# Linear attention's last stage on one core: queries against kv one head at a time, and the product with z on GpSimd

## The chip, the core and the metric

The kernel runs on one core of a Trainium2 chip. A core has TensorE (matrix products, 128 rows by 128 columns, results in PSUM), VectorE, ScalarE, GpSimd and SyncE, which here issues the DMAs. SBUF and PSUM have 128 partitions; PSUM has eight banks of 512 f32 per partition. The metric is the time of one execution on the device in microseconds, as the median over several runs. The profile comes from one execution of its own.

## The reference

One layer on x of 2048 tokens by 1024 channels: a layer norm, then a linear attention with 32 heads of 32 channels, gated by a SwiGLU block on the same normed input.

```python
q, k, v = split(xn @ wqkv)                       # 32 heads of 32
pq, pk = q @ w_phi[h], k @ w_phi[h]              # per head, 32 x 32
phi_q = concat(softmax(pq), softmax(-pq))        # 64 features a head
phi_k = concat(softmax(pk), softmax(-pk))
kv = phi_k^T v ; z = sum_s phi_k                 # per head: 64 x 32 and 64
num = phi_q @ kv ; den = phi_q . z + 1e-6
s = (num / den) heads together @ wo
g = silu((silu(xn @ w1) * (xn @ w3)) @ w2)
out = x + s * g
```

All values are f32.

## The kernel before, in words

The stages follow one another on the same engines. First x is normed, transposed and prepared, and `w_phi` is folded into the query and key weights. Then come the gate's first products (L482), the keys and values (L562), the gate's second product (L751), and last the queries with the attention and its output product. All large products are made in three passes of `float32r` (a value is split into a high part by ScalarE and a low remainder by VectorE, function `split`, L84); a few small products are in plain f32.

**Keys.** In `heads` the keys' features are made by `features` and `scaled`, and `kv` (L547) multiplies them with the values: a head takes 32 columns of the array, four heads lie side by side on the 128 rows of tokens, and the sums stand in the PSUM tile `pkv`. The values carry columns of ones, so that z comes out beside kv. `kv_out` (L594) stores both to DRAM for each half c of the heads (16 heads), in two pairs of DMAs, one for softmax(p) and one for softmax(-p).

**Turning point.** While the gate's second product ends, the kernel loads z, spread over all partitions, into `zb`, and kv into `kvs` (L821 to L831). GpSimd clears `kv_bd` and copies the 32x32 blocks onto its diagonals: four heads in a 128x128 block, for each sign s and half c. SyncE, ScalarE, VectorE and GpSimd follow the order of the program around this place (`in_order`); TensorE does not.

**Queries.** The last loop (L920) goes over 16 token tiles of 128. For tile i it projects the first half (`project_q`, 24 passes at L95), makes its features and weights (`queries`, L876), then runs `attend` (L891) for both halves of tile i-1, projects the second half of tile i, makes its `queries`, and ends tile i-1 with `finish` (L908): the product with `wo`, times the gate, plus x. The order of the instructions on each engine is not that of the text from the second tile on: `in_order()` without an argument hands it to the framework's planner, which simulates durations and places what is ready by the program's priority. Each engine runs its queue in order.

In `queries`, VectorE takes the maximum and minimum of each head (L103, L104), subtracts in both directions (L106, L107), ScalarE takes the exponent (L109), VectorE sums (L112), multiplies with z (L881, two halves s), sums again (L882), works out the reciprocals and scales e (L118). The tile e is laid out by sign s, then head.

In `attend`, four 128x128 transposes for each s put e's features on partitions (L896, into four PSUM banks with tags kv0 to kv3), ScalarE copies them to `et` (L898), and eight matmuls (L903) multiply with `kv_bd`, for each group g of four heads the two signs adding up. The result, four heads of 32 channels on the partitions for each g, stands in one bank `po`. `split` takes it to `oT`: ScalarE the high part (L86), VectorE the low part (L87). `po` has one buffer, so the second `attend` writes it when both have been taken.

Of the kernel before, what the change touches and what calls it, by code (L numbers as in the profile page):

```python
# [8 lines left out]
F = mybir.dt.float32  # L9
R = mybir.dt.float32r  # L10
AF = mybir.ActivationFunctionType
OP = mybir.AluOpType
# [5 lines left out]
P = 128  # L18
# [9 lines left out]
def tile_kernel(ctx: ExitStack, tc: tile.TileContext, x, wkT, wqT, wv, wphi, wo, w1, w3, w2, out):  # L28
# [46 lines left out]
    wk_d = [[dram.tile([P, 512], F, name=f"wk_d{c}_{k}") for k in range(ND)] for c in range(2)]  # L75
    wq_d = [[dram.tile([P, 512], F, name=f"wq_d{c}_{k}") for k in range(ND)] for c in range(2)]
    wo_d = dram.tile([D, D], F, name="wo_d")
    kv_d = dram.tile([P, 4, 4, DH], F, name="kv_d")
    z_d = dram.tile([1, 2, D], F, name="z_d")


    PASSES = ((0, 0), (0, 1), (1, 0))
# [1 line left out]
    def split(hi, lo, src, by=None):  # L84

        nc.scalar.copy(hi, src)  # L86
        (by or nc.vector).tensor_sub(lo, src, hi.bitcast(F))  # L87
# [28 lines left out]
    def scaled(e, by):  # L116
        e3 = e.rearrange("p s (h f) -> p (s h) f", f=DH)
        nc.vector.tensor_mul(e3, e3, by.unsqueeze(2).to_broadcast([P, H, DH]))  # L118
# [475 lines left out]
    def kv_out(c, pkv):  # L594
        kva = work.tile([P, 8, DH], F, name="kva", tag="w")
        zs = small.tile([P, 8], F, name="zs")
        nc.scalar.copy(kva, pkv[:, :, :DH])
        nc.vector.tensor_copy(zs, pkv[:, :, DH])
        for s in range(2):
            nc.sync.dma_start(kv_d[:, 2 * s + c], kva[:, 4 * s:4 * s + 4])  # L600
            nc.sync.dma_start(z_d[0, s, c * 512:(c + 1) * 512].rearrange("(g p) -> p g", p=P), zs[:, 4 * s:4 * s + 4])

    for d, b, t in hs:
        store_h(d, b, t)
# [36 lines left out]
    def stage(k):  # L641
        return ra.tile([P, 4, 512], F, name=f"ra{k % 2}")
# [126 lines left out]
    for r, new in enumerate(steps):  # L769
        kb, i = new or (NKB, 0)  # L770
        end = kb == NKB - 1
        if new is None:
            in_order(ENG.SP, ENG.Activation, ENG.DVE, ENG.Pool)
        if kb + 1 < NKB:
            if i == 2:
                rw = b_load(kb + 1)
            elif i == 3:
                t2 = [b_start(rw, 0)]
            elif i == 4:
                t2.append(b_start(rw, 1))  # L780
            elif i == 5:
                bos[kb + 1] = b_prep(rw, t2, BNAMES[:1], {})
            elif i == 6:
                b_prep(rw, t2, BNAMES[1:2], bos[kb + 1])
        parts = first
        if r + 1 < len(steps) - 1:
            first = a_first(*steps[r + 1])
        bank = {}
        for b, an, bn in TURN:
            if an in FIRST:  # L790
                if new:
                    product(kb, i, bank, parts[2], b, an, bn)
                    if i + 1 == len(pairs) and not end and an == "A11":
                        b_prep(rw, t2, ["T2"], bos[kb + 1])
            elif old:
                product(*old, banks, second, b, an, bn)
                if new and i == 0 and an in ("S3", "S4"):
                    b_prep(rw, t2, ["B22" if an == "S3" else "T4"], bos[kb])
                if not new:
                    k = 2 * (BNAMES.index(bn) - 2)  # L800
                    load_wo(k)
                    load_wo(k + 1)
        if new:
            second = a_second(*parts)
            if i + 1 == len(pairs):
                if end:
                    for k in range(4, 8):
                        load_r(wq, (1, k), wq_d[1][k])
                    for k in range(2):
                        load_wo(k)  # L810
                else:
                    b_prep(rw, t2, ["T1", "T3"], bos[kb + 1])


        if end:
            if i:
                gate(*pairs[i - 1])
            if 0 < i < 5:
                load_r(wq, (1, i - 1), wq_d[1][i - 1])
                split_r(wq[1, i - 1])  # L820
            if i == 2:  # L821
                zb = stage(0)
                nc.sync.dma_start(zb, z_d.rearrange("o s (c n) -> o (s c) n", c=2).to_broadcast([P, 4, 512]))
                kvs = work.tile([P, 4, 4, DH], F, name="kvs", tag="w")
                nc.sync.dma_start(kvs, kv_d)
                kv_bd = stage(1)
                nc.gpsimd.memset(kv_bd, 0.0)
            if 2 < i < 7:
                for j in range(4):
                    sl = slice(32 * j, 32 * j + 32)  # L830
                    nc.gpsimd.tensor_copy(kv_bd[sl, i - 3].rearrange("p (g d) -> p g d", d=P)[:, :, sl], kvs[sl, i - 3])  # L831
            if i == 4:
                close("acca")
                wqp = pool("wq0", 1, side="right")
                for k in range(ND):
                    load_r(wq, (0, k), wq_d[0][k], wqp.tile([P, 2, 512], R, name=f"wq0_{k}"))
            if i == 6:
                xf = load_q(0)
            if 4 < i:
                for k in range(3 * (i - 5), min(3 * (i - 4), ND)):  # L840
                    split_r(wq[0, k])
        old, banks = new, bank
# [31 lines left out]
    in_order(ENG.SP)  # L874

    def queries(p, c):  # L876
        e = acc_late.tile([P, 2, 512], F, name="e", tag="acc0", bufs=3)
        r, rf = features(e, small, p)
        ez = acc_late.tile([P, 2, 512], F, name="ez", tag="acc1", bufs=3)
        for s in range(2):  # L880
            nc.vector.tensor_mul(ez[:, s], e[:, s], zb[:, 2 * s + c])  # L881
        nc.vector.tensor_reduce(rf[:, 1, :], ez.rearrange("p s (h f) -> p (s h) f", f=DH), axis=AX.X, op=OP.add)  # L882
        nc.vector.tensor_mul(rf[:, 1, :], rf[:, 1, :], rf[:, 0, :])
        den = small.tile([P, 16], F, name="den")
        nc.vector.scalar_tensor_tensor(den, r[:, 1, 0, :], 1e-6, r[:, 1, 1, :], op0=OP.add, op1=OP.add)
        nc.vector.reciprocal(den, den)
        nc.vector.tensor_mul(r[:, 2], r[:, 0], den.unsqueeze(1).to_broadcast([P, 2, 16]))
        scaled(e, rf[:, 2, :])
        return e

    def attend(c, e):  # L891
        eT = []
        for s in range(2):
            pt = ps.tile([P, 4, P], F, name="pt2", tag=f"kv{2 * c + s}", bufs=1)
            for g in range(4):
                nc.tensor.transpose(pt[:, g, :], e[:, s, g * P:(g + 1) * P], ident)  # L896
            et = work.tile([P, 4, P], F, name="et", tag="w")
            nc.scalar.copy(et, pt)  # L898
            eT.append(et)
        po = ps.tile([P, 4, P], F, name="po", tag="tr", bufs=1)  # L900
        for g in range(4):
            for s in range(2):
                nc.tensor.matmul(po[:, g, :], kv_bd[:, 2 * s + c, g * P:(g + 1) * P], eT[s][:, g, :], start=s == 0, stop=s == 1)  # L903
        oT = wp.tile([P, 4, 2, P], R, name="oT", bufs=2)
        split(oT[:, :, 0, :], oT[:, :, 1, :], po)
        return oT

    def finish(i, oT):  # L908
# [71 lines left out]
```

## Time and profile before

| | |
|---|---|
| time, median of 3 runs | 2517.87 us (2516.3 to 2518.39) |
| the profiled execution | 2517.11 us, of which the profile's span is 2515.2 us |
| TensorE busy | 2443.6 us, 97% of the span |
| VectorE, ScalarE, GpSimd busy | 1738.6, 903.9, 596.6 us |
| TensorE's clock granted | 0.995 over the span |
| stage of queries and attention | about 2064 us to the end |

Times in the profile are microseconds from the span's start. PE is TensorE's matmul part and PEld its loading of weights, DVE is VectorE, ACT ScalarE, POOL GpSimd, SPq SyncE's queue of DMA issues. A row of the timeline has its start, its length, engine, line, operation, the tile written and those read, shapes and the number of instructions merged into it; square brackets hold idle time ahead of it and what ended that. A matmul's length holds the way through the array, so lengths of neighbouring rows overlap and starts tell more than lengths. A plain f32 matmul shows as two records. A busy TensorE need not be at its peak rate.

### The profile page before, as it was taken

Reading aid. Unit: us, or ns where it says so; the run is one execution under the profiler, and the core shown is the slowest. Engines: PE = TensorE matmul, PEld = TensorE weight load, DVE = VectorE, ACT = ScalarE, POOL = GpSimd, SP = SyncE. Lnnn points to the kernel's source line nnn. Section 1 sums busy time; section 2 is a strip of 40 time slices with the busy share of each in tenths; the row PEclk is TensorE's granted clock in tenths of the full one; section 3 lists DMA queues with packets and bytes.
Section 4 is the critical chain, followed back from the end, with each engine's and each line's share of the span. In section 5 each row is a group of like instructions: output and inputs, shape, how many; then the busy total and the mean of one; then the engine's idle time right before and its main releaser. Section 6 shows DMA issues by size and latency. Waiting matters only on the chain.

```text
span 2515.2 us, 34167 instructions
## 1 busy us (share of the span) xinstructions
PE 2443.6 (97%) x13136; PEld 2018.4 (80%) x13136; DVE 1738.6 (69%) x2635; ACT 903.9 (36%) x1593; POOL 596.6 (24%) x468
## 2 busy tenths in 40 slices
PE   6999999999999999999999989999999999999999
PEld 5888788888788888887887877888877877888887
DVE  8576766764444444443555568999999989777775
ACT  6455444433333333331111125443333453222221
POOL 1244444432222232220000002223333220100100
PEclk9999999999999999999999999999999999999999
DMA  8779887765632322338769623222122372222221
GB/s 298 235 247 296 286 249 258 249 215 173 195 105 80 101 80 72 93 138 327 268 193 328 210 86 85 92 84 89 54 92 97 109 247 85 73 92 68 76 76 67
DMA packets 260179, 394.02 MB, mean 157 GB/s; under 512 B 17712, under 2 KB 165680, under 8 KB 257968
## 3 DMA queue, kind: packets, MB, share of 16 engines
q1 hardware_dynamic: 260016, 391.84, 47.7%
q8 instruction: 103, 1.69, 0.3%
q14 instruction: 60, 0.49, 0.1%
HBM read 269.88 MB, written 126.10 MB: 157 GB/s over the span
## 4 chain that ended last, share of the span: by engine, by line
PE 78%; DVE 9%; DMA 3%; ACT 1%; issue 1%; SPq 1%; ACTq 0%; DVEq 0%
PE bankb L482 21%; PE pm L95 13%; PE bankc L482 10%; PE bankb L751 7%; PE bankb L562 7%; PE banka L482 5%; PE bankc L751 3%; PE bankc L562 3%; PE po L903 2%; DVE acc L763 2%; DVE bo L87 2%; PE banka L562 2%; PE banka L751 2%; DVE aos L87 1%; DMA ra<-in_w 1%
## 5 line engine op out<-in xcount | busy, mean ns | idle before, releaser
L87 DVE TENSOR_TENSOR bo<-rw,bo 128x512 fp32r<-128x512 f32 x336 | 267.2, 796 | 183.4 <-ACT bo L86 182.3
L86 ACT CAST bo<-rw 128x512 fp32r<-128x512 f32 x336 | 200.1, 621 | 16.2 <-PE bankb L482 3.5
L261 POOL TENSOR_TENSOR rw<-rw,t 128x512 f32<-128x512 f32 x56 | 77.0, 1375 | 539.9 <-DVE bo L87 539.7
L751 PE MATMUL bankb<-bo,aos 128*128 128x512 f32 x672 | 172.6, 392 | 9.7 <-DVE acc L763 8.6
L751 PE MATMUL bankc<-bo,aos 128*128 128x512 f32 x672 | 171.4, 390 | 5.1 <-DVE bo L87 2.3
L751 PE MATMUL bankb<-bo,aof 128*128 128x512 f32 x672 | 173.3, 394 | 0.0
L482 PE MATMUL bankb<-op0S,bo 128*128 128x512 f32 x672 | 163.3, 392 | 4.9 <-ACT u L498 3.8
L482 PE MATMUL bankb<-op0A,bo 128*128 128x512 f32 x672 | 160.6, 392 | 7.1 <-ACT bo L86 4.5
L761 POOL TENSOR_TENSOR acc<-acc,u 128x512 f32<-128x512 f32 x48 | 78.2, 1629 | 362.3 <-ACT u L760 333.6
L482 PE MATMUL bankc<-op0S,bo 128*128 128x512 f32 x672 | 162.6, 391 | 0.4 <-ACT u L505 0.4
L482 PE MATMUL bankc<-op1S,bo 128*128 128x512 f32 x672 | 161.5, 390 | 0.7 <-issue 0.7
L482 PE MATMUL bankb<-op1A,bo 128*128 128x512 f32 x672 | 158.8, 392 | 3.4 <-DMA op1A<-xo_d1A 3.4
L482 PE MATMUL bankb<-op1S,bo 128*128 128x512 f32 x672 | 161.4, 389 | 0.0
L751 PEld LDWEIGHTS bankb<-bo,aos 128*128 128x128 f32 x672 | 125.0, 188 | 40.7 <-DVE acc L763 13.9
L482 PEld LDWEIGHTS bankb<-op0A,bo 128*128 128x128 f32 x672 | 125.5, 188 | 34.3 <-ACT bo L86 4.7
L751 PEld LDWEIGHTS bankc<-bo,aos 128*128 128x128 f32 x672 | 125.9, 188 | 32.8 <-DVE bo L87 2.6
L482 PEld LDWEIGHTS bankb<-op1A,bo 128*128 128x128 f32 x672 | 127.3, 189 | 30.3 <-issue 3.8
L482 PEld LDWEIGHTS bankb<-op0S,bo 128*128 128x128 f32 x672 | 125.1, 188 | 32.5 <-ACT u L498 5.4
L751 PEld LDWEIGHTS bankb<-bo,aof 128*128 128x128 f32 x672 | 127.9, 190 | 26.8
L482 PEld LDWEIGHTS bankc<-op1S,bo 128*128 128x128 f32 x672 | 126.1, 188 | 27.2 <-issue 1.1
L482 PEld LDWEIGHTS bankb<-op1S,bo 128*128 128x128 f32 x672 | 126.2, 188 | 26.2
L482 PEld LDWEIGHTS bankc<-op0S,bo 128*128 128x128 f32 x672 | 125.7, 188 | 26.6 <-ACT u L505 0.8
(193 smaller groups left out, 4833.1 us busy)
## 6 DMA issues: line engine op xcount, KB each, us to landing
rw<-in_w SPq DMA_DIRECT2D x112, 512.0 KB, 5.1
h_d<-h SPq DMA_DIRECT2D x112, 256.0 KB, 6.2
hr<-h_d SPq DMA_DIRECT2D x56, 512.0 KB, 3.2
xoS<-xo_d0S SPq DMA_DIRECT2D x32, 512.0 KB, 8.3
xoS<-xo_d1S SPq DMA_DIRECT2D x32, 512.0 KB, 3.9
ra<-in_w SPq DMA_DIRECT2D x14, 1024.0 KB, 6.9
xoA<-xo_d0A SPq DMA_DIRECT2D x24, 512.0 KB, 8.1
xoA<-xo_d1A SPq DMA_DIRECT2D x24, 512.0 KB, 3.9
```

The costliest lines, as they stand in the source:

```text
L86: nc.scalar.copy(hi, src)
L87: (by or nc.vector).tensor_sub(lo, src, hi.bitcast(F))
L95: nc.tensor.matmul(p, xT[dch][:, a], w(dch, b), start=n == 0, stop=n == 3 * ND - 1)
L261: nc.gpsimd.tensor_sub(b11, b22, t2)
L482: nc.tensor.matmul(bank[b], bo[bn][:, w, k], ao[an][:, u, k], start=first and n == 0, stop=LAST[b] == an and n == 11, skip_group_check=True)
L562: nc.tensor.matmul(bank[b], xo[an][:, u, k], wb[bn][:, w, k], start=an in ("A11", "A12", "S1") and n == 0, stop=LAST[b] == an and n == 11, ...
L751: nc.tensor.matmul(bank[b], ao[:, u, POS[an] + k], bos[kb][bn, k][:, w], start=first and n == 0, stop=LAST[b] == an and n == 5, skip_group ...
L761: nc.gpsimd.tensor_add(c, c, u)
L763: nc.vector.tensor_add(c, pb, c)
L903: nc.tensor.matmul(po[:, g, :], kv_bd[:, 2 * s + c, g * P:(g + 1) * P], eT[s][:, g, :], start=s == 0, stop=s == 1)
```

## The change

Four things go together.

- The layout of kv and z. In DRAM kv becomes `[2, 2, DH, 2*G, DH]`: by a head's place in its pair, sign and feature, then by pair, so that on loading one head's 64 features (both signs) stand in one half of the 128 partitions. `kvu` is this tile; nothing is cleared or copied for it. z is stored by half, head and sign. `kv_out` issues one DMA for each sign and each of the four heads on a strip of 32 partitions, for kv and for z: 16 where there were 4. The 1e-6 of the denominator is added into z's first-sign part.
- `queries` lays e out by head, then sign. The product with z becomes one instruction of 128x1024 on GpSimd. The two softmax sums of a head are brought to a common form: with rho the ratio of the two sums, the weights are 1/(z-sum of the first sign + rho times z-sum of the second) and rho times that.
- `attend` transposes four 128-column chunks q at a time, each with two heads of 64 features. For each chunk and each of its two heads one matmul takes 64 rows (the half hh of the array's rows) and 32 columns (the strip g), with 128 columns of queries: 16 matmuls of one head where there were 8 of four heads and one sign. No sums are carried over instructions. `po` has two banks, one per row half. The transposes use three rotating banks (tag `tr`) instead of four.
- `wo`'s rows are put in the order in which the heads now come out, on the host, ahead of the launch.

```diff
-    kv_d = dram.tile([P, 4, 4, DH], F, name="kv_d")
-    z_d = dram.tile([1, 2, D], F, name="z_d")
+    kv_d = dram.tile([2, 2, DH, 2 * G, DH], F, name="kv_d")
+    z_d = dram.tile([1, 2, 4, 4, 2, DH], F, name="z_d")
...
-        nc.vector.tensor_copy(zs, pkv[:, :, DH])
+        nc.vector.tensor_scalar_add(zs[:, :4], pkv[:, :4, DH], 1e-6)
+        nc.vector.tensor_copy(zs[:, 4:], pkv[:, 4:, DH])
         for s in range(2):
-            nc.sync.dma_start(kv_d[:, 2 * s + c], kva[:, 4 * s:4 * s + 4])
-            nc.sync.dma_start(z_d[0, s, c * 512:(c + 1) * 512].rearrange("(g p) -> p g", p=P), zs[:, 4 * s:4 * s + 4])
+            for j in range(4):
+                sl = slice(32 * j, 32 * j + 32)
+                nc.sync.dma_start(kv_d[j % 2, s, :, G * c + j // 2:G * c + G:2], kva[sl, 4 * s:4 * s + 4])
+                nc.sync.dma_start(z_d[0, c, :, j, s].rearrange("g f -> f g"), zs[sl, 4 * s:4 * s + 4])
...
-                zb = stage(0)
-                nc.sync.dma_start(zb, z_d.rearrange("o s (c n) -> o (s c) n", c=2).to_broadcast([P, 4, 512]))
-                kvs = work.tile([P, 4, 4, DH], F, name="kvs", tag="w")
-                nc.sync.dma_start(kvs, kv_d)
-                kv_bd = stage(1)
-                nc.gpsimd.memset(kv_bd, 0.0)
-            if 2 < i < 7:
-                for j in range(4):
-                    sl = slice(32 * j, 32 * j + 32)
-                    nc.gpsimd.tensor_copy(kv_bd[sl, i - 3].rearrange("p (g d) -> p g d", d=P)[:, :, sl], kvs[sl, i - 3])
+                zb = flat(stage(0))
+                nc.sync.dma_start(zb, z_d.rearrange("o c g j s f -> o (c g j s f)").to_broadcast([P, 2 * D]))
+                kvu = flat(stage(1))[:, :2 * G * DH].rearrange("p (g d) -> p g d", d=DH)
+                nc.sync.dma_start(kvu, kv_d.rearrange("a s f g d -> (a s f) g d"))
...
     def queries(p, c):
...
+        nc.scalar.activation(ef, ef, AF.Exp)
+        nc.gpsimd.tensor_mul(ez, ef, zb[:, c * 2 * 512:(c + 1) * 2 * 512])
...
+        nc.vector.tensor_reduce(sums[:, 0].rearrange("p h s -> p (h s)"), e3, axis=AX.X, op=OP.add)
+        nc.vector.reciprocal(t[:, 0], sums[:, 0, :, 1])
+        nc.vector.tensor_mul(t[:, 0], sums[:, 0, :, 0], t[:, 0])
+        nc.vector.tensor_reduce(sums[:, 1].rearrange("p h s -> p (h s)"), ez.rearrange("p (h f) -> p h f", f=DH),
+                                axis=AX.X, op=OP.add)
+        nc.vector.tensor_mul(t[:, 1], sums[:, 1, :, 1], t[:, 0])
+        nc.vector.tensor_add(t[:, 1], t[:, 1], sums[:, 1, :, 0])
+        nc.vector.reciprocal(by[:, :, 0], t[:, 1])
+        nc.vector.tensor_mul(by[:, :, 1], by[:, :, 0], t[:, 0])
+        nc.vector.tensor_mul(e3, e3, by.rearrange("p h s -> p (h s)").unsqueeze(2).to_broadcast([P, H, DH]))
...
     def attend(c, e):
+        po = ps.tile([P, 2, 512], F, name="po", tag="po", bufs=1)
+        for q in range(2):
+            pt = ps.tile([P, 4, P], F, name="pt2", tag="tr", bufs=3)
             for g in range(4):
-                nc.tensor.transpose(pt[:, g, :], e[:, s, g * P:(g + 1) * P], ident)
+                nc.tensor.transpose(pt[:, g, :], e[:, (4 * q + g) * P:(4 * q + g + 1) * P], ident)
             et = work.tile([P, 4, P], F, name="et", tag="w")
             nc.scalar.copy(et, pt)
-            eT.append(et)
-        po = ps.tile([P, 4, P], F, name="po", tag="tr", bufs=1)
-        for g in range(4):
-            for s in range(2):
-                nc.tensor.matmul(po[:, g, :], kv_bd[:, 2 * s + c, g * P:(g + 1) * P], eT[s][:, g, :], start=s == 0, stop=s == 1)
+            for g in range(4):
+                for hh in range(2):
+                    sl = slice(64 * hh, 64 * hh + 64)
+                    nc.tensor.matmul(po[32 * g:32 * g + 32, hh, q * P:(q + 1) * P], kvu[sl, G * c + 4 * q + g], et[sl, g],
+                                     start=True, stop=True, skip_group_check=True)
         oT = wp.tile([P, 4, 2, P], R, name="oT", bufs=2)
-        split(oT[:, :, 0, :], oT[:, :, 1, :], po)
+        o4 = oT.rearrange("p (h q) u t -> p h q u t", q=2)
+        split(o4[:, :, :, 0], o4[:, :, :, 1], po[:, :, :2 * P].rearrange("p h (q t) -> p h q t", t=P))
...
-        "wo": np.asarray(A_wo),
+        "wo": np.asarray(A_wo).reshape(2, 2, 4, 2, DH, D).transpose(0, 3, 1, 2, 4, 5).reshape(D, D),
```

More of the change, by code (lines that the diff above doesn't have):

```diff
@@ L876, in queries @@
     def queries(p, c):
-        e = acc_late.tile([P, 2, 512], F, name="e", tag="acc0", bufs=3)
-        r, rf = features(e, small, p)
-        ez = acc_late.tile([P, 2, 512], F, name="ez", tag="acc1", bufs=3)
-        for s in range(2):
[L881 to L889, printed above, removed]
+        e = acc_late.tile([P, 16, 2, DH], F, name="e", tag="acc0", bufs=3)
+        ez = acc_late.tile([P, 2 * 512], F, name="ez", tag="acc1", bufs=3)
+        mm = small.tile([P, 2, 16], F, name="mm2")
+        p3 = p.rearrange("p (h f) -> p h f", f=DH)
@@ new lines, in queries @@
+        nc.vector.tensor_reduce(mm[:, 0, :], p3, axis=AX.X, op=OP.max)
+        nc.vector.tensor_reduce(mm[:, 1, :], p3, axis=AX.X, op=OP.min)
+        nc.vector.tensor_sub(e[:, :, 0], p3, mm[:, 0, :].unsqueeze(2).to_broadcast([P, 16, DH]))
+        nc.vector.tensor_sub(e[:, :, 1], mm[:, 1, :].unsqueeze(2).to_broadcast([P, 16, DH]), p3)
+        ef = e.rearrange("p h s f -> p (h s f)")
+        e3 = e.rearrange("p h s f -> p (h s) f")
+        nc.scalar.activation(ef, ef, AF.Exp)
+        nc.gpsimd.tensor_mul(ez, ef, zb[:, c * 2 * 512:(c + 1) * 2 * 512])
@@ new lines, in queries @@
+        sums = small.tile([P, 2, 16, 2], F, name="sums")
+        by = small.tile([P, 16, 2], F, name="by")
+        t = small.tile([P, 2, 16], F, name="rho")
+        nc.vector.tensor_reduce(sums[:, 0].rearrange("p h s -> p (h s)"), e3, axis=AX.X, op=OP.add)
[3 more added lines that the diff above has]
+                                axis=AX.X, op=OP.add)
@@ L891, in attend @@
+        nc.vector.tensor_mul(t[:, 1], sums[:, 1, :, 1], t[:, 0])
[3 more added lines that the diff above has]
+        nc.vector.tensor_mul(e3, e3, by.rearrange("p h s -> p (h s)").unsqueeze(2).to_broadcast([P, H, DH]))
+        return ef
     def attend(c, e):
-        eT = []
-        for s in range(2):
-            pt = ps.tile([P, 4, P], F, name="pt2", tag=f"kv{2 * c + s}", bufs=1)
+        po = ps.tile([P, 2, 512], F, name="po", tag="po", bufs=1)
@@ L901, in attend @@
-        for g in range(4):
-            for s in range(2):
-                nc.tensor.matmul(po[:, g, :], kv_bd[:, 2 * s + c, g * P:(g + 1) * P], eT[s][:, g, :], start=s == 0, stop=s == 1)
+            for g in range(4):
[3 more added lines that the diff above has]
+                                     start=True, stop=True, skip_group_check=True)
```

## The prediction

> **What bounds the kernel now.** I read the page first for the busy shares, then the busy time by stage, then TensorE's timeline over one token tile of the last stage, and last the groups and waits of that stage. The page and the table by stage (time, then busy time and instruction count of PE, PEld, DVE, ACT, POOL, then clock and DMA):
>
> ```profile
> span 2515.2 us, 34167 instructions
> PE 2443.6 (97%) x13136; PEld 2018.4 (80%) x13136; DVE 1738.6 (69%) x2635; ACT 903.9 (36%) x1593; POOL 596.6 (24%) x468
> ...
> 2300.00:2500.00 200.00, 199.16 (x1062) 169.69 (x1060) 148.87 (x249) 48.73 (x83) 19.23 (x15) 1.00 0.23 77
> ```
>
> In the stage that the change edits, TensorE is busy 199.2 of 200 us and VectorE 148.9. One period of it, TensorE alone:
>
> ```profile
> 2300.57 5.61 PE L95 MATMUL pm<-wq,xh 128*128 128x512 f32 x24
> 2306.01 1.25 PE L896 MATMUL pt<-ident,e 128*128 128x128 f32 x10
> 2307.34 0.49 PE L903 MATMUL po<-et,ra 128*128 128x128 f32 x2
> 2307.66 0.38 PE L896 MATMUL pt<-ident,e 128*128 128x128 f32 x2
> 2307.88 1.78 PE L903 MATMUL po<-et,ra 128*128 128x128 f32 x14
> 2309.49 0.60 PE L896 MATMUL pt<-ident,e 128*128 128x128 f32 x4
> 2309.85 3.91 PE L95 MATMUL pm<-bo,xh 128*128 128x512 f32 x16
> 2313.59 1.95 PE L903 MATMUL po<-et,ra 128*128 128x128 f32 x16
> 2315.30 2.07 PE L95 MATMUL pm<-bo,xh 128*128 128x512 f32 x8
> ...
> 2328.09 5.61 PE L95 MATMUL pm<-wq,xh 128*128 128x512 f32 x24
> ```
>
> From one first projection to the next are 2328.09 - 2300.57 = 27.52 us, and no row waits. So what TensorE does not do here comes off the time, and what VectorE does not do is worth nothing unless TensorE waits for it. The 16 records of one `attend` at L903 run from 2313.59 to 2315.30: 1.71 us, 107 ns each. In the whole run:
>
> ```profile
> L903 PE MATMUL po<-et,ra x512: 269/275/378, 2087.5 to 2500.2; 128*128 128x128 f32 x171
> ```
>
> 512 records are 32 calls of `attend` (16 tiles, two halves), in all 32 x 1.71 = 54.7 us. Each matmul of plain f32 has two records: 8 matmuls, 16 records per call.
>
> **The change, part by part.** *The product with kv.* 8 full-array matmuls per call become 16 of 64 rows by 32 columns, so 32 records, each still with 128 columns of queries to stream. If nothing overlaps, that is 32 x 107 ns = 3.42 us, twice the present. The only row of the trace with small tiles is the key product L547, on 128 rows by 32 columns, four column strips in turn:
>
> ```profile
> 1274.23 2.88 PE L562 MATMUL bankb<-op2T,xoS 128*128 128x512 f32 x12
> 1276.95 2.88 PE L562 MATMUL bankc<-op2T,xoS 128*128 128x512 f32 x12
> 1279.76 0.77 PE L547 MATMUL pkv<-v,e 128*32 128x34 f32 x64
> 1280.50 1.86 PE L562 MATMUL bankb<-op2T,xoS 128*128 128x512 f32 x7
> ...
> L547 PE MATMUL pkv<-v,e x128: 192/197/220, 1279.8 to 1289.4; 128*32 128x34 f32 x128
> ```
>
> Twelve full matmuls take 2.72 us from start to start, so without L547 the next group would have begun at 1279.67; it began at 1280.50, and the block of 64 cost 0.83 us. Of its 0.77 busy, the last record is 0.20 by itself, so the 64 starts lie within 0.57 us: 9.0 ns a record. The remaining 0.26 us is the price of going into small tiles and back. Streaming grows with the columns: 9.0 x 128/34 = 34 ns a record, 1.09 us for a call if the new tiles overlap four at a time as these do. If the two row halves overlap as well, eight at a time, it is half, 0.54 us. No row shows row halves, and the change gives each half its own PSUM bank, so I take 0.8, midway between.
>
> The switch of 0.26 us is paid per block of small matmuls that stands between full ones. The present plan splits one `attend` of a tile by transposes and keeps the other in one piece (rows above), and the new `attend` waits for two copies of `et` in turn. I take 1.5 blocks a call, 0.39 us; the bounds are 1 and 2. Together 0.8 + 0.39 = 1.19 us against 1.71: 0.52 us less a call, **16.6 us** less in 32 calls. Bounds: 0.54 + 0.26 = 0.80 (29 us less) and 1.09 + 0.52 = 1.61 (3 us less).
>
> The Trainium skill ("TensorE: Matmul & The Clock Gate", Part 3) puts tiles of different row and column groups at some 4 ns behind one another and lists 16 of them at 10.6 times the speed, which speaks for the eight-fold end. Its page "TensorEngine Tiling (Array Packing)", Key Properties, says that a change of tiling mode drains the array, and its Gotcha 1 that row tiles may not share a bank; L547's 0.26 us agrees with the drain, and no row here tests the second. By the skill the saving would be that of the second rival below; by the row alone it would be 1.71 - 1.09 - 0.39 = 0.23 us a call, 7 us.
>
> *The product with z.* These groups are from the last 415 us (count, busy, mean ns, then idle before and its releaser), the pairs below from the timeline:
>
> ```profile
> L916 POOL TENSOR_TENSOR gx<-gx 128x512 f32<-128x512 f32 x30 | 38.4, 1283 | 399.9 <-DVE gx L915 399.9
> L881 DVE TENSOR_TENSOR ez<-e,ra 128x512 f32<-128x512 f32 x58 | 38.0, 655 | 0.0
> L112 DVE TENSOR_REDUCE r<-e 128x32 f32<-128x1024 f32 x29 | 35.4, 1220 | 22.9 <-ACT e L109 22.9
> ...
> 2308.73 1.06 ACT L109 ACTIVATE e<-e 128x1024 f32<-128x1024 f32 x1
> 2309.69 0.59 ACT L86 CAST oT<-po 128x512 fp32r<-128x512 f32 x1
> 2309.82 1.22 DVE L112 TENSOR_REDUCE r<-e 128x32 f32<-128x1024 f32 x1 [1.12 <-ACT e L109]
> 2312.36 0.68 DVE L87 TENSOR_TENSOR oT<-po,oT 128x512 fp32r<-128x512 f32 x1
> 2314.85 0.17 DVE L885 SCALAR_TENSOR_TENSOR den<-r 128x16 f32<-128x16 f32 x1
> 2325.57 1.29 POOL L916 TENSOR_TENSOR gx<-gx 128x512 f32<-128x512 f32 x1 [22.47 <-DVE gx L915]
> 2325.63 1.26 DVE L885 SCALAR_TENSOR_TENSOR den<-r 128x16 f32<-128x16 f32 x1
> ```
>
> VectorE loses 2 x 0.655 = 1.31 us per `queries`, 42 us in 32 calls, all beside a full TensorE: worth 0. GpSimd gains one product of 128x1024, an estimate of 2 x 1.283 = 2.57 us from L916. It is idle for 400 of these 415 us, so the work fits. What counts is latency: VectorE's second sum must wait for GpSimd. Exp ends at 2309.79, GpSimd would end at 2312.4, while the first sum ends at 2311.0 and two small operations follow; some 1.1 us of waiting replaces 1.31 us of work. Six small operations replace five. So the chain of one `queries` is as long as before. Its consumer, the transposes of the next tile, has a whole tile's time for the first half. Queued behind the waiting sum on VectorE are the small operations, the scaling of e, the low half of `oT` and the low halves of `xh`. Taken as 0; the danger is the third rival.
>
> *Buffers and banks.* The transposes go from four banks to three rotating ones, `po` from one bank to two (still one buffer); 16 transposes and four copies of the same size per tile remain. TensorE's order is set by a plan whose durations need not be those of the chip. Today it leaves no gap; a new plan may. From 0 to the third rival's 22 us, I take 2.
>
> *Storing and loading kv and z.* `kv_out` issues 16 DMAs per column half instead of 4. At its second call SyncE's queue shows:
>
> ```profile
> 1507.98 0.32 SPq L600 DMA_DIRECT2D kv_d<-kva  x1
> 1508.48 0.64 SPq L601 DMA_DIRECT2D z_d<-zs  x1
> 1509.17 0.49 SPq L600 DMA_DIRECT2D kv_d<-kva  x1
> 1509.72 0.42 SPq L601 DMA_DIRECT2D z_d<-zs  x1
> 1512.94 0.32 SPq L690 DMA_DIRECT2D hr<-h_d  x1
> ...
> 1523.59 0.62 ACT L86 CAST aof<-hr 128x512 fp32r<-128x512 f32 x1 [1.11 <-DMA hr<-h_d]
> ```
>
> Four issues take 1.87 us, so 16 take some 7.5 and end near 1515.5 instead of 1510.1. The `hr` load behind them would go out up to 2.5 us late, and ScalarE already waits 1.11 us for it. Between 0 and 2.5 us, I take 1. The first call lies in the key stage, a whole tile pair ahead of its reader, and costs 0. The GpSimd fill and 16 copies that built `kv_bd` go; they ran while TensorE multiplied, which waits in that stretch for other things, so 0. The reordered `wo` is prepared on the host.
>
> **The sum.** The profiled execution took 2517.11 us (span 2515.2, 1.9 around it), 0.8 below the median of 2517.87. 2517.1 - 16.6 + 1 + 2 = 2503.5; with the 0.8, **2504 us**.
>
> **The rivals.** *No change (2518).* Row halves don't overlap and the plan cuts the small matmuls finer: 1.09 us and 2.4 switches of 0.26 make 1.71, what L903 takes now. For it: the plan's three L903 groups in one tile, one of only two records. Against it: one `attend` is in one piece today.
>
> *Full overlap (2490).* Eight tiles at a time and one block a call: 0.54 + 0.26 = 0.80, 0.91 less a call, 29 us, and 1 back for the DMAs. For it: separate banks, and four-fold overlap already seen. Against it: 32 records of one call still enter in order, two in a row on the same tile.
>
> *VectorE's queue holds `po` (2526), the slower side.* The second `attend`'s matmuls may write `po` only when VectorE has taken the low half of `oT` from it: 2312.36 + 0.68 = 2313.04, and today they start at 2313.59. In the new order the first small product of two sums may stand ahead of that. L885 shows the mechanism: 0.17 us alone, 1.26 when it starts 0.06 us after a GpSimd product, because it cannot run until GpSimd is done. Then `oT` is taken at 2312.4 + 0.1 + 0.7 = 2313.2 while a plan that doesn't know of this has sent TensorE there 1.5 us before; 1.5 us x 15 tiles = 22 us on top of 2504. It decides once the wait is more than the 2 x 0.52 = 1.04 us that a tile gains. For it: that pair of rows. Against it: `oT` is ready at 2309.69 + 0.59 = 2310.28, before the first sum ends, and can be taken right behind it. The Trainium skill ("SBUF — State Buffer", Who interferes with whom) has the rule for it: a VectorE instruction with two SBUF inputs and a GpSimd one that reads SBUF exclude each other. By that rule, the sums and `oT` (from PSUM) are not held themselves, and the trace agrees with 0.17 against 1.26.
>
> *Tiles don't overlap at all (2573).* 3.42 instead of 1.71 us, 32 times: 55 us more. L547's 9 ns a record, where one full pass takes 107 ns for 128 columns, speaks against it.
>
> **Chances and range.** Forecast 0.50 (its own range 2496 to 2512), full overlap 0.17, no change 0.14, held `po` 0.14, no overlap 0.05. About 0.2%, 5 us, is what a measurement here tells from nothing. Faster: 0.67 less a little of the forecast's upper edge, 0.66; the same: 0.14 and that edge, 0.16; slower: 0.18, nearly all of the last two. The range reaches from the full overlap, 2488, to the lower part of the held `po`, 2522; it leaves out some 0.05 below and 0.14 above.
>
> **What would show it.** Right: L903's successor has 1024 records whose groups of 16 or 32 last 0.4 to 0.8 us from start to start, a period near 26.5 us, no idle time ahead of it that names `oT`, GpSimd busy some 82 us more in this stage. Wrong: records 50 ns or more apart (no overlap), a period still at 27.5 with TensorE waiting on VectorE's `oT` ahead of the second `attend` (held `po`), many groups of two to eight small matmuls among transposes (switches), or a later start of the stage at 1510 (DMAs).

## The result, and the profile after

The changed kernel takes 2494.52 us (median, 2493.32 to 2495.56) against 2517.24 (2515.47 to 2518.48) for the kernel before: ratio 0.991, 95% interval 0.9897 to 0.9923. It is faster by 22.7 us, where 13.6 were forecast. The profiled execution took 2493.32 us.

The first rows of the page of the changed kernel:

```profile
span 2491.5 us, 35284 instructions
PE 2417.3 (97%) x13648; PEld 1976.0 (79%) x13648; DVE 1699.8 (68%) x2605; ACT 902.2 (36%) x1593; POOL 671.5 (27%) x483
```

TensorE is busy for 26.3 us less (2443.6 before), VectorE for 38.8 less and GpSimd for 74.9 more. The 512 added records of TensorE (13136 before) are those of the small matmuls, 16 more in each of 32 calls.

TensorE's timeline over one tile of the last stage (start, duration, operation, tiles, count; the changed kernel, at nearly the place that the prediction shows of before):

```profile
2291.41 5.61 PE L95 MATMUL pm<-wq,xh 128*128 128x512 f32 x24
2296.86 1.26 PE L912 MATMUL pt<-ident,e 128*128 128x128 f32 x10
2298.19 0.94 PE L918 MATMUL po<-et,ra 64*32 64x128 f32 x32
2299.06 0.88 PE L912 MATMUL pt<-ident,e 128*128 128x128 f32 x6
2299.69 1.86 PE L95 MATMUL pm<-bo,xh 128*128 128x512 f32 x7
2301.49 0.76 PE L918 MATMUL po<-et,ra 64*32 64x128 f32 x32
2302.18 4.15 PE L95 MATMUL pm<-bo,xh 128*128 128x512 f32 x17
2306.16 6.96 PE L95 MATMUL pm<-bo,oT 128*128 128x512 f32 x30
2312.96 4.24 PE L95 MATMUL pm<-wos,oT 128*128 128x512 f32 x18
2317.04 5.61 PE L95 MATMUL pm<-wq,xh 128*128 128x512 f32 x24
```

From one first projection to the next are now 2317.04 - 2291.41 = 25.63 us; before they were 27.52. No row waits. The second `attend` is one block of 32 records that holds the array from 2301.49 to 2302.18, 0.69 us, where the 16 full records took 1.71. The first one takes 2299.06 - 2298.19 = 0.87 us between transposes, also in one piece.

Where the 23.8 us between the two profiled executions come from is read from the starts of the first projection `pm<-wq,xh` of the tiles. The stage starts at 2063.95 us before and at 2063.96 after, so nothing is gained or lost ahead of it. At the start the second tile's first projection follows at once on the first tile's two, before any `attend`, so it opens no interval of its own: the first interval reaches from the first tile's start to the third's and holds the first tile's two calls of `attend`. Each later interval but the last also holds one pair of calls, the last holds two pairs. In the stage:

| interval | before | after | difference |
|---|---|---|---|
| first (first to third tile) | 38.86 | 43.61 | +4.75 |
| second (third to fourth tile) | 32.70 | 30.04 | -2.66 |
| the twelve after that, each | 27.51 | 25.63 | -1.88 |
| sixteenth tile's start to the last matmul | 44.50 | 41.03 | -3.47 |

Twelve times 1.88 is 22.6; with the other three rows the sum is -23.9 (from the unrounded starts). In the steady tiles one call of `attend` saves 0.94 us, or 30.1 us for all 32. Some 6 us are lost again, nearly all at the stage's start: its first two intervals should have gained 2 x 1.88 = 3.8, and lost 2.1. Where the experiments below speak of the first two tiles, these two intervals are meant.

Rows of that start, from the timeline of the changed kernel; then the rows of the `e` waits in the view of TensorE's waits (us in total, times, longest), for the changed kernel over its whole run and for the kernel before in the first 76 us of the stage:

```profile
2063.96 0.73 PE L95 MATMUL pm<-wq,xh 128*128 128x512 f32 x2
...
2085.16 2.34 POOL L888 TENSOR_TENSOR ez<-e,ra 128x1024 f32<-128x1024 f32 x1 [5.17 <-ACT e L887]
2085.30 3.29 DVE L902 TENSOR_TENSOR e<-e,by 128x1024 f32<-128x1024 f32 x1
...
2088.73 1.94 PE L912 MATMUL pt<-ident,e 128*128 128x128 f32 x8 [3.79 <-DVE e L902]
```

```profile
PE pt L912 <- DVE e L902: 4.8, 3, 3.8
```

```profile
PE pt L896 <- DVE e L118: 1.1, 2, 0.9
```

TensorE waits 3.79 us for VectorE's scaling L902 of the first `e`. Its queue has put the transposes after 14 of the 24 passes of the second tile's second half (from 2081.61; after 20 of them before), so the other ten stand behind the wait. Scaling `e` took 1.22 us at this place before (timeline of the kernel before):

```profile
2084.83 1.22 DVE L118 TENSOR_TENSOR e<-e,r 128x1024 f32<-128x1024 f32 x1
```

Now it takes 3.29, because GpSimd is in the middle of the product for the other half: L888 ends at 2085.16 + 2.34 = 2087.50, and L902 1.09 us after that, at 2088.59, which is a little less than its own undisturbed duration. The Trainium skill ("SBUF — State Buffer", Who interferes with whom) says that a VectorE instruction with two SBUF inputs and a GpSimd one that reads SBUF exclude each other. These rows agree: the wait is paid whole, not shared. TensorE's waits in the first two intervals, added up along its timeline, come to 3.1 us before and 7.6 after, so 4.4 of the 5.9 us are waits.

The rest fits the granted clock. The same stretch before and after (time, then busy time and instruction count of PE, PEld, DVE, ACT, POOL, then granted clock, DMA share, GB/s):

```profile
2087.40:2094.20 6.80, 6.35 (x33) 4.63 (x32) 6.80 (x15) 2.18 (x4) 0.00 (x0) 1.00 0.13 39
2087.40:2094.20 6.80, 5.47 (x46) 4.20 (x47) 6.24 (x13) 2.71 (x4) 0.44 (x2) 0.50 0.11 34
```

In the changed kernel TensorE was granted half its clock from late in the 3.79 us wait until 2094.2. The nine passes from 2092.07 take 2095.25 - 2092.07 = 3.18 us there, where nine at the 0.227 us a pass of the steady tiles take 2.04.

### The profile page after: what moved, and what is told of

Same layout as the page of the kernel before. It is cut to its first block, busy times and chain, and to the rows that moved or that the text cites. A ratio compares the mean times of both kernels' runs of the same rounds, so it can differ in the third digit from the quotient of the medians.

```text
span 2491.5 us, 35284 instructions
## 1 busy us (share of the span) xinstructions
PE 2417.3 (97%) x13648; PEld 1976.0 (79%) x13648; DVE 1699.8 (68%) x2605; ACT 902.2 (36%) x1593; POOL 671.5 (27%) x483
```

## The experiments

The theory after the result: the product with kv in small tiles gives the gain, at some 0.94 us a call; the product with z on GpSimd gives none, and costs some 6 us at the stage's start, by the two profiled executions above. The rivals: the relief of VectorE is part of the gain; or the switch into small tiles is a different share of the 0.79 us than it seems, so that the streaming is dearer.

**z back on VectorE.** The change without its GpSimd part:

```
-        nc.gpsimd.tensor_mul(ez, ef, zb[:, c * 2 * 512:(c + 1) * 2 * 512])
+        nc.vector.tensor_mul(ez, ef, zb[:, c * 2 * 512:(c + 1) * 2 * 512])
```

> The changed kernel with the product with z back on VectorE, as one instruction of 128x1024; everything else of the change kept. Theory: the gain comes from TensorE's small tiles alone, and VectorE's relief is worth nothing. Then a token tile still takes 25.6 us from first projection to first projection, TensorE's 3.8 us of waiting for e in the first tile goes (there VectorE's scaling of e took 3.29 us behind GpSimd's product), and the time is 2489 to 2492 us. Rival: VectorE's relief carries part of the gain; then a tile takes over 26 us, TensorE waits for VectorE in each, and the time is above 2500 us.

Measured: 2489.27 us, ratio 0.9896 (0.9879 to 0.9912). The steady tiles are as long as in the changed kernel (25.65), the first two 37.70 and 29.57, together 67.3 us instead of 73.7. That is the 71.6 of before less 2 x 1.88, within 0.5. The `e` waits of TensorE shrink:

```profile
PE pt L912 <- DVE e L902: 1.9, 2, 1.4
```

The same kernel a second time beside other kernels:

> The changed kernel with all products with z on VectorE, a second time, beside the changed kernel on the same chip. Theory: 5 us less than the changed kernel, all of it in the first two tiles of the stage. Rival: the 5 us come from stages ahead, which the edit does not touch but whose length differs from build to build; then its last stage is no shorter than the changed kernel's.

2487.49 us, ratio 0.9881 (0.9865 to 0.9898); first tiles 38.08 and 29.57, steady 25.63. The interval of either ratio overlaps with that of the changed kernel, so the times alone do not settle the 5 to 7 us; the intervals of the stage show the same change in both.

**z on GpSimd alone.** The kernel before, with nothing but that product moved:

```
-            nc.vector.tensor_mul(ez[:, s], e[:, s], zb[:, 2 * s + c])
+            nc.gpsimd.tensor_mul(ez[:, s], e[:, s], zb[:, 2 * s + c])
```

> The kernel before with only the product with z moved to GpSimd, as two instructions of 128x512; attention as before. Theory: a tile stays at 27.5 us, and the time at 2517 to 2523 us, the upper end if the first tile's scaling of e is held by GpSimd as in the changed kernel. Rival: the move by itself carries part of the gain; then the time is under 2512 us.

Measured: 2537.59 us, ratio 1.0084 (1.0069 to 1.0099): slower by 21 us at the median, which neither side had expected. The steady tile takes 28.71 us, 1.2 more than before. The timeline of one tile, then the row that grew in TensorE's waits:

```profile
2354.79 2.55 POOL L881 TENSOR_TENSOR ez<-e,ra 128x512 f32<-128x512 f32 x2 [6.97 <-ACT e L109]
2357.37 1.22 DVE L882 TENSOR_REDUCE r<-ez 128x32 f32<-128x1024 f32 x1 [1.47 <-POOL ez L881]
2358.77 0.63 DVE L87 TENSOR_TENSOR oT<-po,oT 128x512 fp32r<-128x512 f32 x1
2359.45 2.05 PE L903 MATMUL po<-et,ra 128*128 128x128 f32 x16 [0.89 <-DVE oT L87]
```

```profile
PE po L903 <- DVE oT L87: 12.7, 14, 1.1
```

The second sum L882 cannot start until GpSimd is done and idles VectorE for 1.47 us. Behind it in VectorE's order stands the low half of `oT`, which is what frees the one `po` buffer, and TensorE's second `attend` waits for that once a tile: 14 times, 12.7 us. This is the prediction's third rival. It does occur, though not in the changed kernel. In the profiled execution (2541.51 us, the longest of the four) the stage itself is 18.3 us longer than before (first intervals 40.13 and 34.26, last 45.69); the rest lies in stages that the edit does not touch.

**The same with a second `po`.** If that chain is the cause, a second buffer should remove it. The transposes go to three rotating banks to make room:

```
-            pt = ps.tile([P, 4, P], F, name="pt2", tag=f"kv{2 * c + s}", bufs=1)
+            pt = ps.tile([P, 4, P], F, name="pt2", tag="tr", bufs=3)
...
-        po = ps.tile([P, 4, P], F, name="po", tag="tr", bufs=1)
+        po = ps.tile([P, 4, P], F, name="po", tag="po", bufs=2)
```

> The kernel before with the product with z on GpSimd, as in the run that was 21 us slower, and po with two buffers (the transposes rotate over three banks instead of four, which frees the bank). Theory: those 1.2 us a tile are the second attend waiting for po, since VectorE takes the low half of oT only after the sum that waits for GpSimd. With a second po nothing waits for that, and a tile is back at 27.5 us. Rival: VectorE is late as a whole; then a tile stays near 28.7 us and TensorE waits for another of its results.

Measured: 2516.72 us, a single time, where the kernel before takes 2516.55 (median). The timeline of TensorE shows the old period again: from one row to the other are 27.53 us.

```profile
2333.41 1.25 PE L896 MATMUL pt<-ident,e 128*128 128x128 f32 x10
...
2360.94 1.25 PE L896 MATMUL pt<-ident,e 128*128 128x128 f32 x10
```

No wait of `po` on `oT` is left. The held `po` was the cause of the loss in the steady tiles, and with it gone the move of the product to GpSimd is worth nothing there, as the prediction had it: VectorE's relief is not felt. The second interval still takes 34.30 us instead of 32.70.

Why the changed kernel is not caught in this is seen in its timeline, in the order of VectorE (start, duration; in brackets the idle time ahead and its releaser):

```profile
2299.23 0.59 ACT L86 CAST oT<-po 128x512 fp32r<-128x512 f32 x1 [0.61 <-PE po L918]
2299.72 1.06 ACT L887 ACTIVATE e<-e 128x1024 f32<-128x1024 f32 x1
2299.85 0.69 DVE L87 TENSOR_TENSOR oT<-po,oT 128x512 fp32r<-128x512 f32 x1 [0.32 <-ACT oT L86]
2300.81 1.22 DVE L892 TENSOR_REDUCE sums<-e 128x32 f32<-128x1024 f32 x1 [0.27 <-ACT e L887]
```

The small matmuls end before ScalarE starts the exponential, so ScalarE copies `oT` first and VectorE takes the low half ahead of both sums. Before, the exponential went first. `po` is free long before the second `attend` wants it. Each engine runs its queue in order, so it is the planner, with its own durations, that chose this sequence; these rows show what it chose and not why.

**The small product twice.** Each of the 32 records of a call is issued twice, to price the streaming apart from the switch:

```
+            for _ in range(2):
                 for g in range(4):
                     for hh in range(2):
                         ...
```

> The changed kernel with every chunk's 8 small matmuls issued twice in a row into the same place of po, so that a block has 64 records instead of 32 and as many entries into small tiles as before. The difference is streaming alone. Theory: some 15 ns a record, 0.48 us more a call, a tile 26.6 us, and of the 0.89 us that a block costs now some 0.4 is the way in and out. Rival: 27 ns a record and hardly any cost of the switch; then a tile takes 27.4 us.

Measured: 2542.8 us, a single time; the steady tiles take 28.5 to 30.1 us, more than either side had. The timeline, two rows of VectorE and two of TensorE:

```profile
2355.11 1.22 DVE L896 TENSOR_REDUCE sums<-ez 128x32 f32<-128x1024 f32 x1 [1.33 <-POOL ez L888]
2356.41 0.63 DVE L87 TENSOR_TENSOR oT<-po,oT 128x512 fp32r<-128x512 f32 x1
```

```profile
2357.18 1.15 PE L919 MATMUL po<-et,ra 64*32 64x128 f32 x64 [2.20 <-DVE rho L895]
2358.25 3.91 PE L95 MATMUL pm<-bo,xh 128*128 128x512 f32 x9
```

The block of 64 lasts 2358.25 - 2357.18 = 1.07 us, 0.38 more than the block of 32: 12 ns a record. That answers the question. The excess time is the held `po` once more: with the longer first block the plan has ScalarE take the exponential ahead of its copy of `oT`, the low half of `oT` falls behind the second sum, which waits 1.33 us for GpSimd, and TensorE waits 2.20 us. (The view names a small operation that ends 0.07 us after `oT`, at 2356.41 + 0.63 = 2357.04.) Two blocks and the wait account for the shorter tiles: 25.63 + 2 x 0.38 + 2.20 = 28.6 us. In the tiles of 30.1 us TensorE's clock is cut as well: behind the block shown here it is granted 0.55 from 2358.2 to 2361.6, and 1.00 at the same place of the next tile, which takes 28.5. In the changed kernel the copy of `oT` starts at 2299.23 and the exponential at 2299.72; how near its plan came to the other order, no run shows.

**All 128 rows for each head.** A quarter of the columns, but no row halves:

```
-  ... kvu[sl, G * c + 4 * q + g], et[sl, g],
+  ... kvu[:, G * c + 4 * q + g], et[:, g],
```

> The changed kernel with each small matmul on all 128 rows and 32 columns instead of 64 rows and 32 columns; as many instructions, same columns streamed, same banks. It leaves out the separation of the two heads of a pair (each gets the sum of both), so only its time counts. Theory: row halves overlap, eight tiles at a time. Without them only four strips overlap, a block of 32 records takes 0.4 us more (27 ns a record instead of some 15), a tile 26.4 us instead of 25.6, the time some 2506 us. Rival: row halves do not overlap and the records are close for another reason; then a tile stays at 25.6 us.

Measured: 2501.45 us, a single time (before: 2516.63), steady tile 26.21. The block in TensorE's timeline:

```profile
2357.74 1.12 PE L918 MATMUL po<-et,ra 128*32 128x128 f32 x32
2358.79 3.47 PE L95 MATMUL pm<-bo,xh 128*128 128x512 f32 x14
```

It lasts 1.05 us. Its last record takes 0.28 (the mean of L918's single records), so 32 starts lie within 1.12 - 0.28 = 0.84 us: 26 ns a record, against (0.76 - 0.28) / 32 = 15 ns with the row halves, and 12 from the product issued twice. The halves do overlap, and they are worth 0.58 us a tile, near the 0.8 expected.

**One block a tile.** The z product on VectorE, and both halves of a tile in one `attend`: 16 transposes, then 64 small records into one `po` of two banks.

```
...
-            oT = [attend(0, pend[1]), attend(1, pend[2])]
+            oT = attend(pend[1], pend[2])
```

> The changed kernel with the product with z on VectorE and with both halves of a tile in one call of attend: all transposes and copies first, then all 32 small matmuls into one po whose two banks hold both halves. The amount of work is the same; the small matmuls may stand in one block per tile instead of two. Theory: each block between full matmuls costs some 0.4 us besides its streaming, so a tile takes 25.2 us if the plan makes one block, and the time is some 2483 us. Rival: the way in and out costs nothing by itself, or the plan keeps two blocks; then a tile stays at 25.6 us.

Measured: 2488.03 us, ratio 0.9885 (0.987 to 0.99), the same as with two blocks. One tile in TensorE's timeline, then its row in the waits:

```profile
2311.61 5.61 PE L95 MATMUL pm<-wq,xh 128*128 128x512 f32 x24
2317.06 1.99 PE L913 MATMUL pt<-ident,e 128*128 128x128 f32 x16
2318.98 1.33 PE L922 MATMUL po<-et,ra 64*32 64x128 f32 x64
2320.24 5.76 PE L95 MATMUL pm<-bo,xh 128*128 128x512 f32 x24
```

```profile
PE pt L913 <- DVE e L902: 6.6, 2, 4.9
```

The next first projection starts at 2336.71, 25.10 us after 2311.61: a steady tile is shorter by 0.54 us. At the start both `e` are wanted at once; TensorE waits 4.9 us, and the clock granted is 0.50 for 10.2 us from late in that wait on. The first two tiles take 72.3 us instead of 67.7, the last interval 1.0 us more, and most of the gain is spent.

**z on VectorE in the first tiles only.** This tests where the 6 us go:

```
-    def queries(p, c):
+    def queries(p, c, first_tile=False):
...
-        nc.gpsimd.tensor_mul(ez, ...)
+        (nc.vector if first_tile else nc.gpsimd).tensor_mul(ez, ...)
...
```

with `first_tile` true for `i == 0`:

> The changed kernel with the product with z on VectorE for the first token tile alone and on GpSimd for the other 15. Theory: GpSimd costs the changed kernel time only at the start of the stage, where VectorE's scaling of the first e waits behind GpSimd's product for the second half. Then the first two tiles together take some 67 us from first projection to first projection, as with all products on VectorE, instead of 73.7, later tiles 25.6, and the time is 2488 to 2491 us. Rival: the start is longer because the chain of the first tile itself is rearranged; then the first two tiles stay near 73 us and the time at 2494.

Measured: 2492.51 us, ratio 0.9905 (0.9888 to 0.9921); first two tiles 43.22 and 28.88, so 72.1 where 67 was expected. The wait for the first `e` is gone, but the wait for the next one takes its place:

```profile
2090.14 2.39 POOL L888 TENSOR_TENSOR ez<-e,ra 128x1024 f32<-128x1024 f32 x1 [34.02 <-ACT e L887]
2091.22 1.34 DVE L901 TENSOR_TENSOR by<-by,rho 128x16 f32<-128x16 f32 x1
2092.57 1.22 DVE L896 TENSOR_REDUCE sums<-ez 128x32 f32<-128x1024 f32 x1
2093.70 1.22 DVE L902 TENSOR_TENSOR e<-e,by 128x1024 f32<-128x1024 f32 x1
2094.97 1.09 PE L912 MATMUL pt<-ident,e 128*128 128x128 f32 x8 [2.72 <-DVE e L902]
```

The second tile's first product on GpSimd (2090.14 to 2092.53) holds a small operation of the first tile on VectorE, L901, until it ends; the second tile's sum stands next in the queue, and the scaling that TensorE waits for comes after both. Behind this wait, too, the granted clock falls to 0.50, for 6.8 us. With `first_tile` true for `i < 2`:

> The changed kernel with the product with z on VectorE for the first two token tiles and on GpSimd for the other 14. With one tile on VectorE the first wait was gone, but the scaling of e of the first tile's second half still stood behind a small product held by GpSimd's product for the second tile, and behind the sum that waits for that. Theory: without a GpSimd product in the first two tiles both waits go, the first two tiles take 67 to 68 us instead of 72.1 (one tile) and 73.7 (none), and later ones 25.6. Rival: the start is longer for another reason; then the first two tiles stay above 71 us.

Measured: 2488.09 us, ratio 0.988 (0.9865 to 0.9894); 38.68 and 29.57, together 68.3, the rest as in the changed kernel. On the same chip the changed kernel itself:

> The changed kernel itself once more, beside the two runs above on the same chip. Expected at 2494 to 2495 us, 43.6 and 30.0 us for the first two tiles and 25.6 for later ones, so that the two differences are taken on one chip.

2495.09 us, ratio 0.9907 (0.9888 to 0.9927). Its first two tiles took 42.11 and 30.07 us, together 72.2, and not the 73.6 expected: the wait for the first `e` was 3.03 us instead of 3.79, and the half clock lasted 3.4 us instead of 6.8. The medians differ by 7.0 us, but in the profiled executions the first two tiles differ by 72.2 - 68.3 = 3.9; another 2.7 lie ahead of the stage, which starts at 2066.23 and 2063.50. With 73.7 against 67.3 and 67.7 from the pairs above, GpSimd in the first two tiles costs the changed kernel 4 to 6 us. In the other 14 it costs nothing that these intervals show (25.63 in both).

**One block from the second tile on.** The z product on VectorE, the halves of the first tile apart, the others in one block:

```
...
-            oT = [attend(0, pend[1]), attend(1, pend[2])]
+            oT = attend(pend[1:], pend[0] == 0)      # (es, apart)
```

> All products with z on VectorE; attend for the first tile's two halves one after the other, and from the second tile on both halves in one call with one block of small matmuls. Theory: the one block saves 0.54 us a tile as before, and the first two tiles take 67.7 us instead of the 72.3 of the run with one block throughout, where the first product had to wait for both halves of e. Then the time is 2480 to 2484 us. Rival: the one block pushes its wait into the next tile; then the first three tiles together are no shorter than with one block throughout, and the time is 2487.

Measured: 2484.43 us, ratio 0.9868 (0.9853 to 0.9884), the lowest time, clear of the changed kernel on the same chip. The first two tiles take 70.65 us, where 67.7 was expected: 1.6 less than with one block throughout, a third of the gain expected there. Rows of TensorE's timeline 25.10 us apart, and the waits:

```profile
2335.10 5.61 PE L95 MATMUL pm<-wq,xh 128*128 128x512 f32 x24
2342.46 1.33 PE L923 MATMUL po<-et,ra 64*32 64x128 f32 x64
2360.20 1.98 PE L95 MATMUL pm<-wq,xh 128*128 128x512 f32 x8
```

```profile
PE pt L913 <- DVE e L902: 3.0, 3, 1.5
```

Against the versions with z on VectorE and two blocks (2487.5 to 2489.3) its interval overlaps, so that this second step is a gain is likely by the periods, but not settled by the times.

**The clock at the stage's start.** The first two intervals beside the mean clock that TensorE was granted in the first 76 us of the stage:

| kernel | first two intervals, us | clock |
|---|---|---|
| before | 71.6 | 1.00 |
| changed; once more | 73.7; 72.2 | 0.96; 0.98 |
| z on GpSimd alone; with a second `po` | 74.4; 72.9 | 0.98; 1.00 |
| z on VectorE; once more | 67.3; 67.7 | 1.00; 1.00 |
| z on VectorE, first tile; first two | 72.1; 68.3 | 0.96; 1.00 |
| one block; from the second tile on | 72.3; 70.7 | 0.93; 0.96 |

The versions near 68 us kept the full clock. One block from the second tile on shows what the clock alone takes: its waits at the start are those of z on VectorE once more (the longest 1.46 and 1.47 us), but from 2097 to 2103 it was granted 0.50 where the other had 1.00, and twelve passes `pm<-bo,oT` took 5.20 us (from 2098.55) instead of 3.22 (from 2099.75). That is most of the 3.0 us by which it missed the expected 67.7. The lowered stretches last 3.4, 6.8 or 10.2 us and stand in or behind pauses of TensorE, but the same pauses brought one here and none there; what sets them off was not tested. So the 4 to 6 us of GpSimd at the start are longer waits and a lowered clock, and the second part differs between executions of one kernel.

## Why the prediction was right, and where its sizes were off

The direction, its cause (TensorE's time in the product with kv) and the range hold. The size was 13.6 us for 22.7: 2494.52 us is outside the forecast's own 2496 to 2512 and closer to the rival of full overlap (2490) than to the forecast (2504). In the steady tiles that rival was right, with 0.80 us a call for the measured 0.79 (as a total; its parts were 0.54 and 0.26), and z on VectorE comes to its time (2487.5 to 2489.3). What brings the measured time nearer to the forecast is a loss at the stage's start that neither had; that is luck.

- **Streaming, 0.8 us a call: about twice what it is.** The midway point between four and eight tiles at a time failed. The 32 records start within 0.38 us (product issued twice) to 0.48 (the block's own rows). The eight-fold bound was 0.54. The lower bound was itself scaled from L547's 34 columns by the ratio of columns; with four tiles at a time the 128-column records came 26 ns apart, not 34, so time grew less than in proportion to the columns. The Trainium skill ("TensorE: Matmul & The Clock Gate", Part 3) has tiles of different groups some 4 ns behind one another. The runs show the overlap of both halves, but at 12 to 15 ns a record, with the two records that each matmul has here.
- **Switch, 0.26 us a block: too cheap.** The second call costs 0.69 us and some 0.10 of surplus ahead of it: the seven projections take 2301.49 - 2299.69 = 1.80 us, 0.21 more than seven of 0.227 (the 24 from 2291.41 to 2296.86 take 5.45), where a surplus of 0.11 stood before too. Of these 0.79 us, 0.38 to 0.48 is streaming, so 0.3 to 0.4 is the switch. Merging two blocks saved 0.54 a tile, which also bounds it.
- **Blocks, 1.5 a call: there was 1.** Both calls of a tile stay in one piece. 0.4 x 1 at most for 0.26 x 1.5: these two errors cancel. The whole call is 0.79 us in place of 1.19, and the steady saving 0.94 us in place of 0.52.
- **z on GpSimd, 0: right in the steady tiles, wrong at the stage's start.** The groups of the changed kernel from 2100 us on show the product at 2395 ns (2.57 us estimated), and 38.0 us in which VectorE's second sum waited for it, 1.3 a call (1.1 estimated); nothing there reaches TensorE. The step that failed is "its consumer has a whole tile's time": that holds in the steady tiles. In the first tile TensorE comes to the first `e` before it is scaled, and the prediction had only looked at a steady tile. It cost 4 to 6 us, part of it through the lowered clock.

```profile
L888 POOL TENSOR_TENSOR ez<-e,ra 128x1024 f32<-128x1024 f32 x29 | 69.4, 2395 | 197.9 <-issue 119.8 <-ACT e L887 68.8 <-DVE bo L87 9.3
L896 DVE TENSOR_REDUCE sums<-ez 128x32 f32<-128x1024 f32 x29 | 35.4, 1220 | 38.0 <-POOL ez L888 38.0
L918 PE MATMUL po<-et,ra 64*32 64x128 f32 x992 | 25.5, 280 | 1.8 <-ACT et L914 0.3
```

- **Held `po`, the slower rival (2526):** the chain is real. By itself, on the kernel before, the move costs 21 us, 18.3 of them in the stage (the rival had 22). The 1.5 us a tile of the rival, for which the prediction shows no working, was a wait of 0.9 and a tile 1.2 us longer. Its mechanism was a little different: `oT` is behind the second sum that waits for GpSimd's result, not behind a small operation that is locked out. The reason given against it was that `oT` can be taken right behind the first sum; the changed kernel takes it ahead of both. With the product issued twice the order is the other one again, so the small product's shortness is the likely reason for it.
- **The plan's gaps, +2: 0** in the steady tiles. **The DMAs, +1: 0.** The 16 issues take 9.6 us on SyncE's queue (7.5 estimated), and the `hr` load goes out at 1519.28 instead of 1512.94, 6.3 us later where up to 2.5 was predicted (1.6 of that because the first issue goes out later); but ScalarE waits only 0.7 us for it (1.11 before), and the last stage starts when it did. In SyncE's queue of the changed kernel:

```profile
1509.61 0.32 SPq L604 DMA_DIRECT2D kv_d<-kva  x1
...
1518.76 0.43 SPq L605 DMA_DIRECT2D z_d<-zs  x1
1519.28 0.38 SPq L694 DMA_DIRECT2D hr<-h_d  x1
```

With the measured terms the sum is -32 x 0.94 + 6 = -24 us, and the profiled executions differ by 23.8. This is bookkeeping: both terms come from the same two executions.

## What to carry to other kernels

A change of two parts has to be priced part by part and place by place: here everything but the move to GpSimd gained 27 to 29 us, and that move was worth nothing in the steady tiles, cost 4 to 6 at the start of the stage, and by itself, on the old code, 21. Before moving work to another engine, list what stands behind the instruction that will wait for it, and look at the first tiles of a stage separately, where a consumer's slack is missing, with the granted clock beside the waits. When small matmuls stand between full ones, count the blocks as well as the records.

## What the runs showed of the hardware that was not expected

- 32 plain f32 records of 64 rows by 32 columns with 128 columns of data start 12 to 15 ns apart, with 128 rows by 32 columns 26 ns; a full-array record took 107. A block of them between full-array matmuls costs 0.3 to 0.4 us beside its streaming.
- A GpSimd product of 128x1024 held the VectorE operations with two SBUF inputs that met it until it ended, even one of 16 columns: 1.34 us for L901 (0.18 when alone), 3.29 for the scaling that takes 1.22.
- At the start of the stage TensorE was granted 0.50 of its clock for 6.8 us in the changed kernel, for 3.4 in a second execution of it, for 10.2 with one block, and for none before or with z on VectorE throughout and two blocks.
- Stages that were not edited shift by a few microseconds between builds or executions: the last stage starts at 2063.95 us before, 2063.96 after and 2066.23 in the changed kernel's second run, 2066.56 with z on VectorE and 2070.03 with z on GpSimd alone. That is as much as some of the effects here, so the stage's own intervals were compared, not only the whole times.
